# One logit block per attention chunk instead of two, with four of its eight products in the MLP's buffer, and two transpose groups in the first down phase

## The chip, the core and the metric

The kernel runs on one NeuronCore of a Trainium2 chip. The core has five engines, each with an instruction queue of its own that it works through in order: TensorE (PE: matmuls and transposes; the profile shows weight loads apart, as PEld), VectorE (DVE), ScalarE (ACT), GpSimd (POOL) and SyncE (SP). They wait for one another by semaphores. Matmuls read SBUF and write one of eight PSUM banks; ScalarE and VectorE carry results from PSUM to SBUF (an eviction). DMAs are issued from the queues of SP, POOL and ACT. The metric is the device time of one execution, in microseconds (us).

## The reference

It is one transformer block on x of 2048 x 576 (bf16), with layer norms modulated by a condition vector c:

```python
sa, ca, ga, sb, cb, gb = (silu(c) @ w_mod).reshape(6, 576)
h = layernorm(x) * (1 + ca) + sa
x = x + ga * attention(h, wqkv, wo)          # 32 heads of 18; 8 keys: positions s, s-2, ..., s-14
h = layernorm(x) * (1 + cb) + sb
x = x + gb * ((h @ w_gate) * (h @ w_up)) @ w_down   # 576 -> 4608 -> 576
```

Attention is local and dilated: a position looks at itself and at seven earlier ones, two apart. For each of the 8 offsets w the logits of a head are the sum over its 18 features of q times the shifted k; then a softmax over the 8, and the weighted sum of eight shifted v. Positions before the start are masked.

## The kernel before, in words

The 2048 positions are cut into eight chunks of 256 (`CH`). Chunks form the groups [0], [1, 2], [3, 4], [5, 6], [7] for the MLP. For each group TensorE goes through two phases. In the **gate/up** phase (`gate_up`) it computes, for each f of 36 slices of 128 hidden features, gate and up side by side, each on 64 rows of the array (class `Pair`, matmuls of L746, PSUM tiles `pg` and `pu`). ScalarE evicts them (L797, L798), and VectorE multiplies them into `hh` (L791, L800), which holds the hidden activations: 36 slices of 512 columns. In the **down** phase (`down`) it multiplies `hh` by w_down on the whole array (L961, L966), and the results go out.

Everything else is laid into these phases as background pieces, written as lists of tuples (TensorE time, VectorE time, what it needs, what it marks, how long the mark waits, what to call). The planner `timed` goes along the phase in estimated time and emits the next piece of a list as soon as its need is marked and VectorE's estimated backlog allows it. So the order of instructions on every engine is fixed when the kernel is built; the estimates only decide the order, and semaphores keep the data right. Pieces that don't fit go on into the following down phase (`late`).

While group g is in gate/up, the attention of the chunks of group g+1 runs beside it. For one chunk:

- `b_p` (L486, VectorE): a product, q times the shifted k, 128 x 1280 bf16, one per offset w. Products go to `prod_t`, which has room for four (`product`).
- `b_l` (L495, TensorE): a logit block for four offsets. 20 matmuls by the 0/1 matrix `ind` sum each head's features; four of them run side by side, each on 32 columns of the array. The result `lgT` (256 columns, half a PSUM bank) is copied by ScalarE to `lgs` (L498; a pool with two buffers).
- `b_ltd` (L512, SP queue): a DMA transpose of `lgs` into `lg_t`.
- `softmax_of` (VectorE and ScalarE), `values_of` (`b_mul`, `b_add`: eight multiplies and sums of the shifted v, into `o_sb`), `b_od` or `b_o`, which bring `o_sb` to `oT` by DMA transpose or by TensorE transposes (L561, evicted by ScalarE in L562, L563), and `b_w` (L642, L644), the output projection, which reads `oT`.

So a chunk has two logit blocks, for w = 0 to 3 and 4 to 7; the second four products reuse `prod_t` after the first block has read it. `prod_t` also serves the MLP: `ld_prods` loads two blocks of w_down into it for the down phase, on the POOL queue.

Group 0 is the special one. In its gate/up phase, near the end, stand two groups of ten TensorE transposes: `a_t4` (L333: `xn` of chunk 4 into `tr_pA`, `tr_pB`; ScalarE evicts three pieces into `hT` in L324, VectorE two in L322, and GpSimd then zeroes `hT`'s unused half in L423) and `b_o(1)` (`o_sb` of chunk 1 into `oT`). The down phase of group 0 is planned by `first_down`: it computes q, k and v of chunk 4 from `hT` (`a_q`, L441; `a_v`, L464), the output projection of chunk 1 from `oT`, then chunk 2's values and projection. Its lists start with a mark `h4` (hT ready, 1.5 after the start) and `o1` (oT ready, 1.5).

```python
product(n): k0 = (prod_n[0] % (4 * CH // n)) * KT * n
hhp.tile([P, FT * 2 * CH], BF, name="hh")     # 36 slices x 512 columns, made anew for each group
```

Of the kernel before, what the change touches and what calls it, by code (L numbers as in the profile page):

```python
# [7 lines left out]
BF = mybir.dt.bfloat16  # L8
F32 = mybir.dt.float32
# [9 lines left out]
P = 128  # L19
# [26 lines left out]
def kernel(  # L46
# [20 lines left out]
    def pool(name, bufs, **kw):  # L67
        return ctx.enter_context(tc.tile_pool(name=name, bufs=bufs, **kw))
# [8 lines left out]
    h2p = pool("h2p", 1)  # L77
    vstage = pool("vstage", 4)
    smp = pool("smp", 1)
    lgsp = pool("lgsp", 2)  # L80
    lgp = pool("lgp", 2)
    attnp = pool("attnp", 1)
    vshp = pool("vshp", 2)
# [337 lines left out]
    def a_t4():  # L421
        a_t(4, False)
        nc.gpsimd.memset(aa[4]["hT"][64:, KF, :], 0.0)  # L423
# [58 lines left out]
    def b_p(i, w):  # L482
        b = bb.setdefault(i, dict(prod={}, vsh={}))
        off = HALO - DIL * (W - 1 - w)
        prod = product(CH)
        nc.vector.tensor_tensor(prod, aa[i]["qT"][:], aa[i]["kT"][:, :, off:off + CH], ALU.mult)  # L486
        b["prod"][w] = prod

    def b_l(i, w0):
        b = bb[i]  # L490
        prods = [b["prod"].pop(w0 + c) for c in range(4)]
        lgT = ps([P, CH], F32, "lgT")
        for m in range(KT):
            for c in range(4):
                nc.tensor.matmul(lgT[H * c:H * (c + 1), :], lhsT=ind[:, m, :], rhs=prods[c][:, m, :],  # L495
                                 start=(m == 0), stop=(m == KT - 1), skip_group_check=True)
        lgs = lgsp.tile([P, CH], BF, name="lgs")
        nc.scalar.copy(lgs[:], lgT[:])  # L498
        b.setdefault("lgs", []).append(lgs)

    def b_lt(i):
        b = bb[i]
        b["lg"] = ps([P, ST, W, H], BF, "lg")
        for w0, lgs in zip((0, 4), b.pop("lgs")):
            for j in range(ST):
                nc.tensor.transpose(b["lg"][:, j, w0:w0 + 4, :].rearrange("p w h -> p (w h)"), lgs[:, js(j)], ident[:])

    def b_ltd(i, w0):
        b = bb[i]
        if w0 == 0:  # L510
            b["lg"] = lgp.tile([P, ST, W, H], BF, name="lg_t")
        b["ltd"] = nc.sync.dma_start_transpose(out=b["lg"][:, :, w0:w0 + 4, :].rearrange("p j w h -> p j (w h)"), in_=b["lgs"][w0 // 4][:])  # L512

    def b_exp(i):
        nc.scalar.activation(bb[i]["dd"][:], bb[i]["dd"][:], ACTF.Exp, scale=scale)
# [39 lines left out]
    def b_o(i):  # L555
        pA = ps([P, 4, CH], BF, "oT_pA")
        pB = ps([P, 1, CH], BF, "oT_pB")
        for m in range(KT):
            d = pA[:, m, :] if m < 4 else pB[:, 0, :]
            for j in range(ST):  # L560
                nc.tensor.transpose(d[:, js(j)], o_sb[:, j, m * P:(m + 1) * P], ident[:])  # L561
        nc.scalar.copy(oT[:, 0:4, :], pA[:])  # L562
        nc.scalar.copy(oT[:, 4, :], pB[:, 0, :])  # L563
# [117 lines left out]

    def prods_of(i):
        r = []
        for w in (0, 4):
            r += [(0, 0.82, "", f"p{i}{v}", 1.0, lambda v=v: b_p(i, v)) for v in range(w, w + 4)]
            r += [(0.75, 0, f"p{i}{w + 3}", f"l{i}{w}", 1.0, lambda w=w: b_l(i, w)), (0, 0, f"l{i}{w}", f"t{i}{w}", 9.0 if i == 7 else 6.0, lambda w=w: b_ltd(i, w))]
        return r
# [28 lines left out]

    def attention_of(c1, c2):
        p2, sm = prods_of(c2), softmax_of(c1)
        first = prods_of(c1) + p2[:4] + sm[:1] + p2[4:6] + sm[1:] + p2[6:]
        return first + values_of(c1, c2) + [(0, 0, "", "-", 0, lambda: b_od(c1))] + softmax_of(c2) + values_of(c2)  # L720

    def norm_of(n, after, free, load=None):
# [164 lines left out]
    def names(th):  # L887
        return [p[3] for p in th]
# [415 lines left out]
    def gb_row():  # L1304
# [27 lines left out]
    def first_down(late):  # L1332
        def q(g):
            return (0.53 if g == 2 else 1.07, 0, "h4", "-", 0, lambda: a_q(4, g))

        def v(j):
            return (1.2, 0, "h4", "-", 0, lambda: a_v(4, j))

        def out_1(first):
            return [(0, 0, "", "o1", 1.5, nop), (1.2, 1.35, "o1", "-", 0, lambda: b_w(1, 0)), (1.2, 1.35, "", "x1", 0.5, lambda: b_w(1, 1)),  # L1340
                    (0, 2.5, "", "s1", 0.7, lambda: b_ln(1)), (0, 0, "s1", "n1", 2.3, lambda: b_norm(1)), (0, 0, "n1", "t1", 9.5, lambda: b_td(1)),
                    (0, 1.0, "t1", "-", 0, lambda: (b_mod(1, (3, 4), False), b_mod(1, (0, 1, 2), True)))]
        a4 = [(0, 0, "", "h4", 1.5, lambda: ld_prods(0))]
        o2 = [(0, 0, "o21", "z2", 0.6, nop), (0.55, 0, "z2", "O2", 0.9, lambda: b_o(2)), (1.2, 1.35, "O2", "-", 0, lambda: b_w(2, 0)), (1.2, 1.35, "", "x2", 0.2, lambda: b_w(2, 1)),
              (0, 2.2, "", "s2", 0.7, lambda: b_ln(2)), (0, 1.5, "s2", "n2", 0.2, lambda: b_norm(2)), (0.55, 1.0, "n2", "-", 0, lambda: b_t(2))]
        return [a4, out_1(True), late + [(0, 0, "", "a2", 0.0, nop)] + values_of(2) + o2, [q(0), q(1), q(2), q(3), q(4), v(0), v(1)]]

# [61 lines left out]
```

## Time and profile before

Three runs: 541.29, 543.39 and 544.81 us; median 543.39.

| | |
|---|---|
| Profiled execution | 543.39 us, span 541.7 |
| TensorE busy | 534.3 us, 99% |
| VectorE, ScalarE, GpSimd busy | 316.6, 252.5, 70.7 us |
| Granted TensorE clock | 1.0 |
| Logit blocks' matmuls (L495) | 280, 10.4 us |
| Gate/up phase of group 0 ends, first down phase starts | 96.94 |
| First down phase ends | 127.51 |
| Gate/up phases of groups 1, 2, 3 | 127.51 to 208.20, 248.49 to 328.23, 368.51 to 446.72 |

Times inside an execution count from the start of the span. Lines of the timeline give start and duration of an instruction (or of several alike, merged, "x6"), engine, line of the kernel, operation, what it writes and reads, shapes, and in brackets how long the engine sat idle before it and what ended that. Matmuls are pipelined: one begins before the last one has ended, so what counts is from start to start. "64*128" or "128*32" before the shapes is the part of the array that a matmul uses, rows by columns.

### The profile page before, as it was taken

Reading aid. Unit: us, or ns where it says so; the run is one execution under the profiler, and the core shown is the slowest. Engines: PE = TensorE matmul, PEld = TensorE weight load, DVE = VectorE, ACT = ScalarE, POOL = GpSimd, SP = SyncE. Lnnn points to the kernel's source line nnn. Section 1 sums busy time; section 2 is a strip of 40 time slices with the busy share of each in tenths; the row PEclk is TensorE's granted clock in tenths of the full one; section 3 lists DMA queues with packets and bytes.
Section 4 is the critical chain, followed back from the end, with each engine's and each line's share of the span. In section 5 each row is a group of like instructions: output and inputs, shape, how many; then the busy total and the mean of one; then the engine's idle time right before and its main releaser. Section 6 shows DMA issues by size and latency. Waiting matters only on the chain.

```text
span 541.7 us, 14628 instructions
## 1 busy us (share of the span) xinstructions
PE 534.3 (99%) x6196; PEld 318.6 (59%) x6196; DVE 316.6 (58%) x715; ACT 252.5 (47%) x625; POOL 70.7 (13%) x110
## 2 busy tenths in 40 slices
PE   8999999999999999999999999999999999999997
PEld 4887888657745444555544444555544445558875
DVE  4899787758776768636358896534344924032212
ACT  4766877534656553012655552014555551006630
POOL 8104005012000210111000110110010101110210
PEclk9999999999999999999999999999999999999999
DMA  9999999879762794878344983983395592859730
GB/s 288 284 287 349 337 266 342 293 133 340 257 185 85 232 228 134 227 213 302 114 119 152 242 279 70 205 239 115 95 278 179 153 315 67 245 139 298 261 90 31
DMA packets 94978, 114.67 MB, mean 212 GB/s; under 512 B 28001, under 2 KB 83698, under 8 KB 94786
## 3 DMA queue, kind: packets, MB, share of 16 engines
q1 hardware_dynamic: 83184, 67.14, 44.7%
q0 software_dynamic: 11424, 46.40, 27.7%
q8 instruction: 48, 0.79, 0.6%
q10 hardware_dynamic: 306, 0.21, 0.1%
q14 instruction: 16, 0.13, 0.1%
HBM read 103.29 MB, written 4.74 MB: 199 GB/s over the span
## 4 chain that ended last, share of the span: by engine, by line
PE 97%; DMA 1%; DVE 0%; issue 0%; SPq 0%; ACT 0%
PE pg L746 29%; PE pu L746 23%; PE acc L961 20%; PE pq L441 4%; PE pq L746 3%; PE pw L644 3%; PE accr L966 3%; PE acc L1016 3%; PE lgT L495 2%; PE pv L746 2%; PE pv L464 2%; DMA wmA<-in_w_mod_dram 1%; PE po L599 1%; PE pwj L621 0%; PE accr L1019 0%; PE pwr L642 0%
## 5 line engine op out<-in xcount | busy, mean ns | idle before, releaser
L746 PE MATMUL pu<-h2T,wgu 64*128 64x512 bf16 (+1 forms) x1376 | 264.9, 331 | 0.9 <-issue 0.9
L746 PE MATMUL pg<-h2T,wgu 64*128 64x512 bf16 (+1 forms) x1376 | 265.7, 331 | 0.0
L746 PEld LDWEIGHTS <-wgu 64*128 64x128 bf16 x2752 | 133.9, 94 | 97.0 <-issue 1.1
L797 ACT CAST u_sb<-pu 128x512 bf16<-128x512 f32 (+1 forms) x172 | 85.8, 499 | 142.4 <-PE pg L746 142.2
L800 DVE TENSOR_TENSOR hh<-g_sb,u_sb 128x512 bf16<-128x512 bf16 x136 | 57.5, 424 | 116.2 <-ACT g_sb L798 115.3
L798 ACT CAST g_sb<-pg 128x512 bf16<-128x512 f32 (+1 forms) x172 | 86.8, 505 | 0.0
L961 PE MATMUL acc<-wd,hh 128*128 128x512 bf16 x344 | 86.1, 380 | 0.0
L961 PEld LDWEIGHTS <-hh 128*128 128x128 bf16 x504 | 49.0, 98 | 59.7 <-issue 1.3
L966 PE MATMUL accr<-wd,hh 128*128 128x64 bf16 x344 | 62.4, 193 | 0.0
L746 PE MATMUL pu<-h2T,wgr 64*128 64x512 bf16 (+1 forms) x188 | 61.5, 327 | 0.0
L746 PE MATMUL pg<-h2T,wgr 64*128 64x512 bf16 (+1 forms) x188 | 61.5, 327 | 0.0
L966 PEld LDWEIGHTS <-hh 128*128 128x128 bf16 x504 | 45.8, 98 | 1.9
L174 POOL DMA_DIRECT2D wd<-in_B_w_down_dram x29 | 21.9, 754 | 180.7 <-PE accr L966 100.1
L486 DVE TENSOR_TENSOR prod_t<-qT,kT 128x1280 bf16<-128x1280 bf16 x56 | 43.9, 820 | 1.3 <-ACT kT L817 0.7
L543 DVE TENSOR_TENSOR vsh<-vsh,attn 128x1152 bf16<-128x1152 bf16 x56 | 39.8, 752 | 0.0
L961 PE MATMUL acc<-prod_t,hh 128*128 128x512 bf16 x112 | 28.6, 380 | 0.0
L746 PEld LDWEIGHTS <-wgr 64*128 64x128 bf16 x376 | 18.5, 94 | 16.2 <-issue 3.0
L324 ACT ACTIVATE h2T<-h2T,modc 128x256 bf16<-128x256 bf16 x12 | 6.6, 595 | 41.5 <-DMA h2T<-xn 41.5
L480 POOL DMA_DIRECT2D vsh<-vd x14 | 12.6, 899 | 94.4 <-DVE o_sb L553 84.4
L441 PE MATMUL pq<-hT,wqk 128*128 128x256 bf16 (+1 forms) x225 | 21.7, 251 | 0.1
L746 PE MATMUL pq<-hT,wqk 64*128 64x256 bf16 (+1 forms) x360 | 21.7, 258 | 0.0
L966 PE MATMUL accr<-prod_t,hh 128*128 128x64 bf16 x112 | 21.6, 193 | 0.0
(214 smaller groups left out, 608.1 us busy)
## 6 DMA issues: line engine op xcount, KB each, us to landing
wgu<-in_B_w_gate_dram SPq DMA_DIRECT2D x41, 512.0 KB, 5.6
wgu<-in_B_w_up_dram SPq DMA_DIRECT2D x41, 512.0 KB, 7.1
wd<-in_B_w_down_dram POOLq DMA_DIRECT2D x29, 576.0 KB, 5.0
vsh<-vd POOLq DMA_DIRECT2D x14, 1152.0 KB, 9.8
prod_t<-in_B_w_down_dram POOLq DMA_DIRECT2D x8, 576.0 KB, 8.4
hh<-in_B_w_down_dram POOLq DMA_DIRECT2D x6, 576.0 KB, 7.3
x_t<-in_A_x_dram SPq DMA_DIRECT2D x8, 288.0 KB, 5.6
x_r<-in_A_x_dram SPq DMA_DIRECT2D x8, 288.0 KB, 7.8
```

Source lines behind the costliest of these rows:

```text
L174: return nc.gpsimd.dma_start(wb[:], B_w_down[r0:r0 + FB * P, :].rearrange("(k p) n -> p k n", p=P))
L441: nc.tensor.matmul(pq[:, gi, :], lhsT=wqk[:, kt, m * P:(m + 1) * P], rhs=hT[:, kt, cols], start=(kt == order[0] and not (by_k and gi)), st ...
L486: nc.vector.tensor_tensor(prod, aa[i]["qT"][:], aa[i]["kT"][:, :, off:off + CH], ALU.mult)
L543: nc.vector.tensor_tensor(v, v, at, ALU.mult)
L644: nc.tensor.matmul(pw[:], lhsT=oT[:, m, js(j)], rhs=wo[:, m, 0:512], start=(m == 0), stop=(m == KT - 1))
L746: return nc.tensor.matmul(out, lhsT=lhs, rhs=rhs, start=first, stop=last, skip_group_check=True)
L797: nc.scalar.copy(u[:, c, :], pu)
L798: nc.scalar.copy(g[:, c, :], pg)
L800: return lambda: nc.vector.tensor_tensor(hh[:, f - c:f + 1, :], g, u, ALU.mult)
L961: nc.tensor.matmul(acc[j][:], lhsT=hh[:, f, js(j)], rhs=wb[:, f % FB, 0:512], start=(f == 0), stop=(f == FT - 1))
L966: nc.tensor.matmul(accr[:, j, :], lhsT=hh[:, f, js(j)], rhs=wb[:, f % FB, 512:D], start=(f == 0 and j == 0), stop=(f == FT - 1), skip_grou ...
L1016: nc.tensor.matmul(acc[i][:], lhsT=hh[:, f, js(j)], rhs=wb(f)[:, c0:c1], start=(f == 0), stop=(f == FT - 1))
```

## The change

For chunks 3 to 7 there is one logit block of eight offsets. The products for w = 4 to 7 go to the last 5120 columns of `hh` (`room["hh"]`; slices 26 to 35 of the group that is in gate/up), so eight products can stand at once. `b_l` runs 40 matmuls into one `lgT` of 2 x 256 columns (one PSUM bank) and one copy to `lgs`, which is now one tile for both halves in a pool of one buffer. Both DMA transposes are issued one after the other behind it. The list of pieces has the chunk's softmax as a whole between the first four and the last four products of the group's second chunk. Chunks 1 and 2 keep two blocks, through the new `lgs` tile.

In group 0 the transposes `a_t4` and `b_o(1)` leave the gate/up phase; empty pieces with the marks `x4` and `O1` stay in their places. `a_t4`, with the load of x for chunk 6, now stands at the start of the first down phase in the same piece as `ld_prods(0)`, and `h4` is marked 1.7 after it; `b_o(1)` comes 0.4 after the start, and `o1` 1.9 after that. Chunk 2's `O2` waits 1.1 instead of 0.9.

The diff, by functions:

```diff
-    lgsp = pool("lgsp", 2)
+    lgsp = pool("lgsp", 1)
...
     def b_p(i, w):
-        prod = product(CH)
+        prod = product(CH) if i < 3 or w < 4 else room["hh"][:, (w - 4) * KT * CH:(w - 3) * KT * CH].rearrange("p (k n) -> p k n", k=KT)
...
-    def b_l(i, w0):
+    room = {}
+
+    def b_l(i, w0, quads=1):
         b = bb[i]
...
+        lgT = ps([P, quads, CH], F32, "lgT")
+        for q in range(quads):
+            prods = [b["prod"].pop(w0 + 4 * q + c) for c in range(4)]
+            for m in range(KT):
+                for c in range(4):
+                    nc.tensor.matmul(lgT[H * c:H * (c + 1), q, :], lhsT=ind[:, m, :], rhs=prods[c][:, m, :],
+                                     start=(m == 0), stop=(m == KT - 1), skip_group_check=True)
+        if w0 == 0:
+            b["lgs"] = lgsp.tile([P, 2, CH], BF, name="lgs")
+        nc.scalar.copy(b["lgs"][:, w0 // 4:w0 // 4 + quads, :], lgT[:])
...
     def prods_of(i):
         r = []
+        if i >= 3:
+            r = [(0, 0.82, "", f"p{i}{v}", 1.0, lambda v=v: b_p(i, v)) for v in range(W)]
+            return r + [(1.3, 0, f"p{i}7", f"l{i}", 1.2, lambda: b_l(i, 0, 2)), (0, 0, f"l{i}", f"t{i}4", 9.0 if i == 7 else 6.0, lambda: [b_ltd(i, w) for w in (0, 4)])]
...
     def attention_of(c1, c2):
-        first = prods_of(c1) + p2[:4] + sm[:1] + p2[4:6] + sm[1:] + p2[6:]
+        if c1 < 3:
+            first = prods_of(c1) + p2[:4] + sm[:1] + p2[4:6] + sm[1:] + p2[6:]
+        else:
+            first = prods_of(c1) + p2[:4] + sm + p2[4:]
...
-    first[at] = (0.6, 0, "o11", "-", 0, lambda: b_o(1))
+    first[at] = (0, 0, "o11", "O1", 0, nop)
...
-                                         (0.6, 0, "n4 v3", "x4", 0, lambda: (a_t4(), load_x(6)))],
+                                         (0, 0, "n4 v3", "x4", 0, nop)],
...
         def out_1(first):
-            return [(0, 0, "", "o1", 1.5, nop), (1.2, 1.35, "o1", "-", 0, lambda: b_w(1, 0)), (1.2, 1.35, "", "x1", 0.5, lambda: b_w(1, 1)),
+            return [(0, 0, "", "o0", 0.4, nop), (0.55, 0, "o0", "o1", 1.9, lambda: b_o(1)), (1.2, 1.35, "o1", "-", 0, lambda: b_w(1, 0)), (1.2, 1.35, "", "x1", 0.5, lambda: b_w(1, 1)),
...
-        a4 = [(0, 0, "", "h4", 1.5, lambda: ld_prods(0))]
+        a4 = [(0.6, 0, "", "h4", 1.7, lambda: (a_t4(), load_x(6), ld_prods(0)))]
...
+        room["hh"] = hh_t[:, FT * 2 * CH - 4 * KT * CH:]
```

As built, the changed order on TensorE has five blocks of 40 `lgT` matmuls for chunks 3 to 7; in the first down phase ten transposes of L333 after the first f, ten of L561 after the second, and the first `pq` of chunk 4 after the fourth. On POOL, ACT and DVE the moved evictions, the zeroing and the loads behind it follow at the same place; the eviction of chunk 2's first output half comes ahead of the modulation of chunk 1's `h2T` on VectorE.

More of the change, by code (lines that the diff above doesn't have):

```diff
@@ L484, in b_p @@
         off = HALO - DIL * (W - 1 - w)
-        prod = product(CH)
+        prod = product(CH) if i < 3 or w < 4 else room["hh"][:, (w - 4) * KT * CH:(w - 3) * KT * CH].rearrange("p (k n) -> p k n", k=KT)
         nc.vector.tensor_tensor(prod, aa[i]["qT"][:], aa[i]["kT"][:, :, off:off + CH], ALU.mult)
         b["prod"][w] = prod
-    def b_l(i, w0):
+    room = {}
+    def b_l(i, w0, quads=1):
         b = bb[i]
[L491 to L499, printed above, removed]
+        lgT = ps([P, quads, CH], F32, "lgT")
[8 more added lines that the diff above has]
+        nc.scalar.copy(b["lgs"][:, w0 // 4:w0 // 4 + quads, :], lgT[:])
     def b_lt(i):
@@ L503, in b_lt @@
         b["lg"] = ps([P, ST, W, H], BF, "lg")
-        for w0, lgs in zip((0, 4), b.pop("lgs")):
+        lgs = b.pop("lgs")
+        for w0 in (0, 4):
             for j in range(ST):
-                nc.tensor.transpose(b["lg"][:, j, w0:w0 + 4, :].rearrange("p w h -> p (w h)"), lgs[:, js(j)], ident[:])
+                nc.tensor.transpose(b["lg"][:, j, w0:w0 + 4, :].rearrange("p w h -> p (w h)"), lgs[:, w0 // 4, js(j)], ident[:])
     def b_ltd(i, w0):
@@ L511, in b_ltd @@
             b["lg"] = lgp.tile([P, ST, W, H], BF, name="lg_t")
-        b["ltd"] = nc.sync.dma_start_transpose(out=b["lg"][:, :, w0:w0 + 4, :].rearrange("p j w h -> p j (w h)"), in_=b["lgs"][w0 // 4][:])
+        b["ltd"] = nc.sync.dma_start_transpose(out=b["lg"][:, :, w0:w0 + 4, :].rearrange("p j w h -> p j (w h)"), in_=b["lgs"][:, w0 // 4, :])
     def b_exp(i):
@@ L1339, in out_1 @@
         def out_1(first):
-            return [(0, 0, "", "o1", 1.5, nop), (1.2, 1.35, "o1", "-", 0, lambda: b_w(1, 0)), (1.2, 1.35, "", "x1", 0.5, lambda: b_w(1, 1)),
+            return [(0, 0, "", "o0", 0.4, nop), (0.55, 0, "o0", "o1", 1.9, lambda: b_o(1)), (1.2, 1.35, "o1", "-", 0, lambda: b_w(1, 0)), (1.2, 1.35, "", "x1", 0.5, lambda: b_w(1, 1)),
                     (0, 2.5, "", "s1", 0.7, lambda: b_ln(1)), (0, 0, "s1", "n1", 2.3, lambda: b_norm(1)), (0, 0, "n1", "t1", 9.5, lambda: b_td(1)),
                     (0, 1.0, "t1", "-", 0, lambda: (b_mod(1, (3, 4), False), b_mod(1, (0, 1, 2), True)))]
-        a4 = [(0, 0, "", "h4", 1.5, lambda: ld_prods(0))]
-        o2 = [(0, 0, "o21", "z2", 0.6, nop), (0.55, 0, "z2", "O2", 0.9, lambda: b_o(2)), (1.2, 1.35, "O2", "-", 0, lambda: b_w(2, 0)), (1.2, 1.35, "", "x2", 0.2, lambda: b_w(2, 1)),
+        assert not {"O1", "x4"} & set(names(late))
+        a4 = [(0.6, 0, "", "h4", 1.7, lambda: (a_t4(), load_x(6), ld_prods(0)))]
+        o2 = [(0, 0, "o21", "z2", 0.6, nop), (0.55, 0, "z2", "O2", 1.1, lambda: b_o(2)), (1.2, 1.35, "O2", "-", 0, lambda: b_w(2, 0)), (1.2, 1.35, "", "x2", 0.2, lambda: b_w(2, 1)),
               (0, 2.2, "", "s2", 0.7, lambda: b_ln(2)), (0, 1.5, "s2", "n2", 0.2, lambda: b_norm(2)), (0.55, 1.0, "n2", "-", 0, lambda: b_t(2))]
```

## The prediction

> **What bounds the kernel now.** I read the page first: busy shares and the chain that ended last.
>
> ```profile
> PE 534.3 (99%) x6196; PEld 318.6 (59%) x6196; DVE 316.6 (58%) x715; ACT 252.5 (47%) x625; POOL 70.7 (13%) x110
> ...
> PE 97%; DMA 1%; DVE 0%; issue 0%; SPq 0%; ACT 0%
> ```
>
> TensorE is busy all the time and is the chain; its clock row shows 9s throughout. There is hardly a stall to remove: only TensorE's own time can shrink, or a new wait be added. So I went to TensorE's timeline and looked at what a foreign block costs inside the gate/up phase. First a logit block of chunk 7 (start, duration, engine, line):
>
> ```profile
> 391.56 0.38 PE L746 MATMUL pu<-h2T,wgu 64*128 64x512 bf16 x1
> 391.57 0.38 PE L746 MATMUL pg<-h2T,wgu 64*128 64x512 bf16 x1
> 391.87 0.73 PE L495 MATMUL lgT<-prod_t,ind 128*32 128x256 bf16 x20
> 392.54 0.39 PE L746 MATMUL pg<-h2T,wgr 64*128 64x512 bf16 x1
> ...
> 392.76 0.38 PE L746 MATMUL pg<-h2T,wgu 64*128 64x512 bf16 x1
> ```
>
> Gate and up matmuls start two by two every 0.215 us, but the block starts 0.305 after the last two: 0.09 lost going in. Its 20 matmuls run four side by side, so they are five steps of 256 columns. A 256-column matmul steps by 0.109 (10 of L441 take 98.91 to 100.00), which makes 0.545. The block takes 0.67: about 0.12 lost inside and coming out. Now ten transposes in gate/up, then ten in the first down phase:
>
> ```profile
> 90.83 0.27 PE L746 MATMUL pg<-h2T,wgu 64*128 64x256 bf16 x1
> 91.03 0.51 PE L333 MATMUL tr_pA<-shifts,xn 128*128 128x128 bf16 x6
> 91.38 0.39 PE L333 MATMUL tr_pB<-shifts,xn 128*128 128x128 bf16 x4
> 91.69 0.28 PE L746 MATMUL pg<-h2T,wgr 64*128 64x256 bf16 x1
> ```
>
> ```profile
> 118.99 0.19 PE L966 MATMUL accr<-prod_t,hh 128*128 128x64 bf16 x1
> 119.02 0.61 PE L561 MATMUL oT_pA<-shifts,o_sb 128*128 128x128 bf16 x8
> 119.47 0.28 PE L561 MATMUL oT_pB<-shifts,o_sb 128*128 128x128 bf16 x2
> 119.58 0.38 PE L961 MATMUL acc<-prod_t,hh 128*128 128x512 bf16 x1
> ```
>
> In gate/up, 90.83 to 91.69 is 0.86; less the 0.107 step of its own matmuls, the transposes cost 0.75. In the down phase the same ten cost 0.56, with no loss at either edge. The form column says what differs: gate/up works on 64 rows, the logit block on 32 columns, transposes and down matmuls on the whole 128*128 array. Each change of form costs about 0.1 us.
>
> **The change, part by part.**
>
> *One logit block per chunk (chunks 3 to 7).* The 40 matmuls stay, and one pair of edges goes. Two blocks cost 2 x (0.67 + 0.09) = 1.52, one costs 0.67 + 0.09 + 5 x 0.109 = 1.31: 0.21 saved, five times, 1.05.
>
> *Two transpose groups into the first down phase.* 0.75 - 0.56 = 0.19 to 0.20 each, 0.40 together. **TensorE's own time: -1.45.**
>
> [...] The trace shows about 0.1 per edge.
>
> *The hand-off in the first down phase is new.* Call its start T0 (before: 96.94). The timeline shows the evictions that move (91.66 to 94.45, with their durations), and the end of gate/up on VectorE and ScalarE, which they now stand behind:
>
> ```profile
> 91.66 1.49 ACT L324 ACTIVATE hT<-tr_pA,modc 128x256 bf16<-128x256 bf16 x3
> 91.80 0.73 DVE L322 TENSOR_SCALAR hT<-tr_pB,modc 128x256 bf16<-128x256 bf16 x2 [0.55 <-PE tr_pB L333]
> ...
> 92.64 0.31 POOL L423 MEMSET hT<- 64x256 bf16 x1 [1.23 <-PE pu L746]
> ...
> 93.54 1.06 ACT L562 COPY oT<-oT_pA 128x1024 bf16<-128x1024 bf16 x1
> ...
> 94.45 0.43 ACT L563 COPY oT<-oT_pB 128x256 bf16<-128x256 bf16 x1
> ...
> 96.53 0.43 DVE L800 TENSOR_TENSOR hh<-g_sb,u_sb 128x512 bf16<-128x512 bf16 x1 [2.01 <-ACT g_sb L798]
> ...
> 96.87 1.03 DVE L695 TENSOR_REDUCE ssum<-dd 128x64 f32<-128x512 f32 x1
> ...
> 97.94 0.26 ACT L696 ACTIVATE ssum<-ssum 128x64 f32<-128x64 f32 x1 [0.63 <-DVE ssum L695]
> ...
> 98.64 0.38 ACT L798 CAST g_sb<-pg 128x256 bf16<-128x256 f32 x1
> ```
>
> ScalarE's last g_sb ends at 99.02, T0 + 2.08: it stands behind chunk 2's softmax logarithm, which waits for VectorE. In the changed order the same instructions stand ahead of the moved evictions, so these start at T0 + 2.1. ScalarE's three hT pieces end at T0 + 3.5. VectorE's last hh (0.43) and two hT pieces (0.73) end at T0 + 3.2, and GpSimd's zeroing (0.11 after it, 0.31 long) at T0 + 3.6.
>
> TensorE meanwhile does one f of down matmuls (4, 0.49), hT's transposes (0.56), 0.49, oT's transposes (0.56), two more f (0.98), and arrives at pq at T0 + 3.08. Its third step needs the third piece at 3.30 and its fifth the zeroing at 3.52: about 0.2 late. Then oT: ScalarE's copies end at about T0 + 4.75 (1.06 and 0.43, overlapping a little), and TensorE wants the last of them at 3.08 + 0.2 + 1.09 + 0.12 = 4.5: 0.25 late. **Stall 0.45.** Bounds: 0, if the softmax sum is earlier because ScalarE no longer copies oT ahead of it, and 1.15, if the zeroing also waits for VectorE's next multiply (attn, 0.69). I take 0.45, which is what the rows give.
>
> Behind the waiting instructions: on GpSimd the two prod_t weight loads and one wd load, so they issue at about 99 to 100 instead of 93.14. prod_t is first read at 116.6 and its slowest landing in the trace took 13.5 us, so it is there by 113.4. DMA moved 355 GB/s or more until 105 and nothing from 107 to 109, so the delayed bytes close up. On ScalarE pq's copies are behind (before at 100.20, now about T0 + 4.8, also 100.2); on VectorE chunk 2's value multiplies, which end in o_sb at 116.5 and are next wanted at 119. VectorE's part of the h2T modulation now comes after one output block; it waits for a transpose landing at 123.2 anyway, and its reader is the next phase at 127.5. If any of this cover were gone, its delay would go straight into TensorE.
>
> *Products in hh's end, one lgs buffer, both DMA transposes together: nothing.* The eight multiplies keep their shape (0.82 each). The end of hh is read last in the previous down phase and written late in gate/up, long after the block. One 128x512 copy replaces two of 0.39. The pair of DMA transposes issues in 2 x 1.17, so the second is 1.17 later behind its block, but the softmax maximum that reads it comes well after: chunk 4 issued at 170.32 and was read at 187.52. The one place where VectorE waited for it (1.51, chunk 5, issued 274.58, read 280.42) gains, since that block now comes some 7 us earlier.
>
> *New wait: a block now needs all eight products.* TensorE stands in order behind it. Before, chunk 5's eighth product ended 265.4 because it waited for the first block; now it needs no such wait. By VectorE's order it ends at about 259.8, and the block starts 18 gate/up and 18 pq matmuls (1.94 + 0.98) after the old first one (259.38), at 262.3. Chunk 4: 166.4 against 168.85. The tightest was chunk 6, 288.8 against 289.69; its block comes one f (1.94) earlier, but its products stand one hh multiply earlier too. No stall expected.
>
> **Sum:** -1.45 + 0.45 = -1.0; with the bounds -1.45 to -0.3. The profiled execution took 543.39 (span 541.7 and 1.7 around it), which is also the median, so 542.4, and 541.9 to 543.1 by the bounds.
>
> **Rivals.**
> 1. *Only the way in is saved.* The 0.1 at the end of a block may be its last matmul running out, which any block pays. Then 7 x 0.09 = 0.63 goes and 0.45 comes: 543.2. Against it: in the down phase the transposes end without a tail.
> 2. *Slower: the zeroing on GpSimd.* It is on the path now. If it waits while VectorE does attn (0.69) and the next two multiplies (1.43), it ends at T0 + 3.2 + 2.1 + 0.3 = 5.6 and TensorE stalls 2.1: 543.39 - 1.45 + 2.1 = 544.0. It decides from a stall of 1.45 on. For it: nothing in the trace shows a zeroing beside such a multiply (at 92.64 a reduction ran). Against it: the order puts the zeroing right behind the eviction. [...]
> 3. *A block waits for its eighth product* in several chunks: if product order gains nothing while the block moves up by 1.94, chunk 6's margin of 0.87 becomes a stall of 1.07; in all five, 5.4, that is 543.39 - 1.0 + 5.4 = 547.8. Against it: VectorE sits idle for 1.0 to 2.6 us before most of its hh multiplies there (chunk 5's stretch), so it has room to be early.
> 4. *The merged block changes form between its halves*: 1.05 is not saved, 543.4.
>
> **How the numbers follow.** Forecast 0.68, rival 1 0.10, rival 2 0.12, rival 3 0.05, rival 4 0.05. Runs shown spread from 541.29 to 544.81, so a median can be off by over 1 us: 541.9 less 1.3 gives 540.6, and rival 2's 544.0 with 0.6 gives 544.6. About 1%, 5.4 us, is what a measurement tells from no change; TensorE idles 7 us in all, most of it outside the change, so faster by more is 0.01, slower (rival 3) 0.04, the same 0.95.
>
> **What would show it.** Logit blocks of 40 taking about 1.21 with 0.09 ahead, five of them; gate/up of the first group unbroken after pv; ten transposes at 0.56 in the first down phase; pq there starting some 0.2 late, pwr another 0.25. A gap over 1.45 there, or a wait of TensorE for VectorE at a block, proves me wrong.

## The result and the profile after

The changed kernel takes 540.8 us in the median of 20 runs (539.6 to 543.35), the kernel before 543.5 in the same measurement (541.24 to 544.81). The ratio is 0.9966 with a 95% interval of 0.9952 to 0.9980: 1.85 us less, 1.1 to 2.6. That is close to the difference of the means, 543.0 and 541.1; the medians differ by 2.7. Single runs of either kernel differ by 3.6 to 3.75 us; the last experiments show a part of where that comes from. Measured again (below), the ratio was 0.9976.

Three lines of the page of the changed kernel, its busy times, one DMA queue, and the chain that ended last:

```profile
PE 532.1 (99%) x6196; PEld 319.7 (59%) x6196; DVE 316.7 (59%) x715; ACT 252.6 (47%) x620; POOL 70.7 (13%) x110
...
q8 instruction: 48, 0.79, 0.6%
...
PE 97%; DMA 1%; DVE 0%; SPq 0%; ACT 0%; issue 0%
```

Queue q8 moves instructions, 48 packets and 0.79 MB; it comes up again further down. Nothing of the picture changed: the same 6196 matmuls, TensorE busy 99%, and TensorE is the chain. The profiled execution took 540.11 us (span 538.4), 3.3 less than the one before. To see where, I cut the timeline of TensorE into its phases, from the start of the first matmul of one to that of the next (us):

| | before | after | difference |
|---|---|---|---|
| set-up | 48.56 | 47.90 | -0.66 |
| gate/up of group 0, up to chunk 3's last v | 39.43 | 38.04 | -1.39 |
| the rest of it, where the transposes stood | 8.95 | 7.41 | -1.54 |
| first down phase | 30.57 | 31.96 | +1.39 |
| gate/up of groups 1, 2, 3 | 80.69, 79.74, 78.21 | 80.25, 79.30, 77.99 | -0.44, -0.44, -0.22 |
| all other phases | | | 0 to 0.01 |

Three rows are the change: -1.54, +1.39 and -1.10, together **-1.25**. The first two rows, -2.05, hold nothing that the change does to TensorE: its order there is the same, and matched matmul by matmul the two traces drift apart where matmuls wait for loads in the set-up, and at two gaps of before. One, at 62.2 inside a logit block, costs 0.25; the other is 1.2 us long in the middle of gate/up, at 69.4, where no engine is named as the cause:

```profile
69.42 0.27 PE L746 MATMUL pg<-h2T,wgu 64*128 64x256 bf16 x1
70.63 0.27 PE L746 MATMUL pu<-h2T,wgu 64*128 64x256 bf16 x1 [0.95 <-issue]
```

The trace after has neither gap. Why it had one and the other not is taken up in the last experiments.

Now the two places that the prediction spoke of. The logit block of chunk 7 after the change, on TensorE's timeline:

```profile
392.37 0.38 PE L756 MATMUL pu<-h2T,wgu 64*128 64x512 bf16 x1
392.37 0.38 PE L756 MATMUL pg<-h2T,wgu 64*128 64x512 bf16 x1
392.68 0.73 PE L498 MATMUL lgT<-prod_t,ind 128*32 128x256 bf16 x20
393.23 0.72 PE L498 MATMUL lgT<-hh,ind 128*32 128x256 bf16 x20
393.88 0.39 PE L756 MATMUL pg<-h2T,wgr 64*128 64x512 bf16 x1
```

The first 20 matmuls read `prod_t`, the second 20 the end of `hh`. They start 0.55 apart, five steps of 0.11, with nothing between the halves. The block begins 0.31 after the last gate/up pair, where pairs follow each other every 0.215, and takes 1.20 where two blocks took 0.67 each. All five blocks of 40 look like this.

And the hand-off in the first down phase, which now starts at T0 = 93.35:

```profile
93.05 1.03 DVE L702 TENSOR_REDUCE ssum<-dd 128x64 f32<-128x512 f32 x1
93.35 0.39 PE L971 MATMUL acc<-wd,hh 128*128 128x512 bf16 x1
...
93.85 0.50 PE L333 MATMUL tr_pA<-shifts,xn 128*128 128x128 bf16 x6
...
94.90 0.61 PE L565 MATMUL oT_pA<-shifts,o_sb 128*128 128x128 bf16 x8
95.09 1.49 ACT L324 ACTIVATE hT<-tr_pA,modc 128x256 bf16<-128x256 bf16 x3
...
95.58 0.72 DVE L322 TENSOR_SCALAR hT<-tr_pB,modc 128x256 bf16<-128x256 bf16 x2
...
96.22 0.68 DVE L710 TENSOR_TENSOR attn<-dd,rs 128x512 bf16<-128x512 f32 x1
96.41 0.31 POOL L423 MEMSET hT<- 64x256 bf16 x1 [6.36 <-PE oT_pB L565]
...
96.44 1.25 PE L441 MATMUL pq<-hT,wqk 128*128 128x256 bf16 x10
...
97.34 0.42 ACT L567 COPY oT<-oT_pB 128x256 bf16<-128x256 bf16 x1
...
97.54 0.48 PE L646 MATMUL pwr<-wo,oT 128*128 128x64 bf16 x5
...
97.85 1.24 PE L648 MATMUL pw<-wo,oT 128*128 128x512 bf16 x5
97.99 2.10 DVE L547 TENSOR_TENSOR vsh<-vsh,attn 128x1152 bf16<-128x1152 bf16 x3 [1.09 <-DMA vsh<-vd]
...
100.00 0.22 DVE L650 TENSOR_TENSOR x<-pwr,ga_bc 128x64 bf16<-128x64 f32 x1
100.02 0.31 PE L646 MATMUL pwr<-wo,oT 128*128 128x64 bf16 x5
...
100.27 1.24 PE L648 MATMUL pw<-wo,oT 128*128 128x512 bf16 x5
```

pq starts at T0 + 3.09 and takes 1.10, as it did before (1.09): it isn't late. Its third step comes at 96.66, 0.08 after ScalarE's third piece of hT; its fifth at 96.88, 0.16 after the zeroing. The first `pwr` and `pw` take 1.39 instead of 1.23, because the last step of `pwr` waits for ScalarE's copy that ends at 97.76: 0.16. The second pair takes 1.33 instead of 1.23, because `pw` waits for VectorE's `x<-pwr` of the first, which ends at 100.22, 0.05 before `pw` starts: 0.10. (In two traces below, where this wait is longer, the profile names that instruction.) That `x<-pwr` stands behind three value multiplies, and these waited 1.09 for a load, `vsh<-vd`. Before the change only two multiplies stood ahead of it.

### The profile page after: what moved, and what is told of

It is laid out like the page before. It is cut to its first block, busy times and chain, and to the rows that moved or that the text cites. A ratio compares the mean times of both kernels' runs of the same rounds, so it can differ in the third digit from the quotient of the medians.

```text
span 538.4 us, 14603 instructions
## 1 busy us (share of the span) xinstructions
PE 532.1 (99%) x6196; PEld 319.7 (59%) x6196; DVE 316.7 (59%) x715; ACT 252.6 (47%) x620; POOL 70.7 (13%) x110
## 4 chain that ended last, share of the span: by engine, by line
PE 97%; DMA 1%; DVE 0%; SPq 0%; ACT 0%; issue 0%
PE pg L756 29%; PE pu L756 23%; PE acc L971 20%; PE pq L441 4%; PE pq L756 3%; PE pw L648 3%; PE accr L976 3%; PE acc L1026 3%; PE pv L756 2%; PE pv L464 2%; PE lgT L498 2%; DMA wmA<-in_w_mod_dram 1%; PE po L603 1%; PE pwj L625 0%; PE pwr L646 0%; PE accr L1029 0%
## 5 line engine op out<-in xcount | busy, mean ns | idle before, releaser
L486 DVE TENSOR_TENSOR prod_t<-qT,kT 128x1280 bf16<-128x1280 bf16 x36 | 28.2, 818 | 3.5 <-ACT kT L827 2.7
```

## The experiments

Each was timed beside the kernel before. Phases are read from each trace as above. "Value multiply" is the start of chunk 2's first `vsh` multiply in the first down phase, counted from T0.

| kernel | ratio to before, 95% | gate/up of groups 1, 2, 3 | first down phase | value multiply |
|---|---|---|---|---|
| before | | 80.69, 79.74, 78.21 | 30.57 | 3.17 |
| after | 0.9966 (0.9952 to 0.9980) | 80.25, 79.30, 77.99 | 31.96 | 4.64 |
| logits only | 0.9965 (0.9941 to 0.9988) | 80.32, 79.30, 77.99 | 30.57 | 3.16 |
| moves only | 0.9985 (0.9966 to 1.0003) | 80.69, 79.74, 78.20 | 31.85 | 4.42 |
| eight products, two blocks | 0.9991 (0.9971 to 1.0011) | 80.69, 79.74, 78.21 | 31.86 | 3.58 |
| two blocks back to back | 0.9987 (0.9968 to 1.0006) | 80.25, 79.29, 77.99 | 31.85 | 4.29 |
| copy on VectorE | 0.9975 (0.9956 to 0.9995) | 80.25, 79.29, 77.99 | 32.11 | 4.79 |
| zeroing seven times | 1.0019 (0.9998 to 1.0040) | 80.25, 79.30, 77.99 | 33.76 | 4.25 |
| after, stream moved by 64 | 1.0019 (1.0001 to 1.0038) | 80.25, 79.30, 77.99 | 31.87 | 3.59 |
| before, stream moved by 64 | 1.0040 (1.0022 to 1.0059) | 80.69, 79.74, 78.20 | 30.57 | 3.16 |
| after, moved by 128 | 1.0006 (0.9987 to 1.0025) | 80.25, 79.30, 77.99 | 31.84 | 3.56 |
| before, moved by 128 | 1.0021 (1.0004 to 1.0038) | 80.69, 79.74, 78.20 | 30.57 | 3.16 |
| after, moved by 192 | 1.0021 (1.0000 to 1.0041) | 80.25, 79.30, 77.99 | 35.81 | 6.96 |
| after, again | 0.9976 (0.9956 to 0.9995) | 80.25, 79.30, 77.98 | 31.86 | 3.58 |

The ratios are uncertain by about 1 us, more than a single step of this change. The gate/up phases of groups 1 to 3 repeat to 0.02 wherever the order is the same, but for the 80.32 of logits only, so they decide between theories, and the ratios only say what all of it is worth.

### Each half of the change alone

Logits only: the transposes go back to the gate/up phase of group 0.

```diff
-    first[at] = (0, 0, "o11", "O1", 0, nop)
+    first[at] = (0.6, 0, "o11", "-", 0, lambda: b_o(1))
...
-                                         (0, 0, "n4 v3", "x4", 0, nop)],
+                                         (0.6, 0, "n4 v3", "x4", 0, lambda: (a_t4(), load_x(6)))],
...
-        a4 = [(0.6, 0, "", "h4", 1.7, lambda: (a_t4(), load_x(6), ld_prods(0)))]
+        a4 = [(0, 0, "", "h4", 1.5, lambda: ld_prods(0))]
...
```

The first down phase's list of the output projection, and `O2`'s 0.9, are those of before too.

> The changed kernel with both transpose groups put back into the gate/up phase of group 0; merged logit blocks stay. Edge theory: every merged block saves one pair of form changes, 0.21 us, so the gate/up phases of groups 1, 2 and 3 take 80.25, 79.29 and 77.99 us as in the changed kernel (80.69, 79.74 and 78.21 before), 1.1 less together, and the end of group 0 and its down phase take what they took before (8.95 and 30.57). Whole time 1.1 below the kernel before. Rival (the gain needs both parts, since the hand-off also moves group 1's start): groups 1 to 3 gain less than 0.9 together.

Moves only: the kernel before, with its two blocks per chunk, and the opposite edit.

```diff
-    first[at] = (0.6, 0, "o11", "-", 0, lambda: b_o(1))
+    first[at] = (0, 0, "o11", "O1", 0, nop)
...
-        a4 = [(0, 0, "", "h4", 1.5, lambda: ld_prods(0))]
+        a4 = [(0.6, 0, "", "h4", 1.7, lambda: (a_t4(), load_x(6), ld_prods(0)))]
...
```

> The kernel before with both transpose groups moved into the first down phase; two logit blocks per chunk as before. Edge theory: gate/up's end takes 7.41 instead of 8.95, the first down phase 31.96 instead of 30.57 (1.13 of transposes and 0.26 of waiting for the output projection's operand and bank), so 0.15 net, and groups 1 to 3 take 80.69, 79.74 and 78.21 as before. Whole time 0.1 to 0.2 below the kernel before, not to be told from none. Rival (the whole time fell by more than the phases show, so the moves gain elsewhere): 0.7 or more below the kernel before.

The two halves don't touch each other. Logits only gains 0.37, 0.44 and 0.22 in the three gate/up phases and leaves the first down phase at 30.57, as before. Moves only has the old gate/up phases, and group 0 as in the changed kernel: 7.41 for the rest of its gate/up, 31.85 for the down phase. So the moves are worth 1.54 - 1.28 = 0.26 us here, and 0.15 in the profiled run after, where the second output projection waited 0.10. The logit blocks carry the change: with them alone the median was 540.68, against 540.8 for all of it in another session.

### What in the merged block gains: the edges, VectorE's freedom or the bank

Eight products, two blocks: the products and the buffer as changed, but each half of the logits is its own block as soon as its four products are there.

```diff
-            r = [(0, 0.82, "", f"p{i}{v}", 1.0, lambda v=v: b_p(i, v)) for v in range(W)]
-            return r + [(1.3, 0, f"p{i}7", f"l{i}", 1.2, lambda: b_l(i, 0, 2)), (0, 0, f"l{i}", f"t{i}4", 9.0 if i == 7 else 6.0, lambda: [b_ltd(i, w) for w in (0, 4)])]
+            for w in (0, 4):
+                r += [(0, 0.82, "", f"p{i}{v}", 1.0, lambda v=v: b_p(i, v)) for v in range(w, w + 4)]
+                r += [(0.75, 0, f"p{i}{w + 3}", f"l{i}{w}", 1.2, lambda w=w: b_l(i, w))]
+            return r + [(0, 0, f"l{i}4", f"t{i}4", 9.0 if i == 7 else 6.0, lambda: [b_ltd(i, w) for w in (0, 4)])]
```

> The changed kernel, eight products and one copy target as there, but the logit block of chunks 3 to 7 in two pieces of 20 matmuls again, with gate/up work between. Edge theory: five pairs of edges come back, so groups 1 to 3 take 80.67, 79.71 and 78.20, 1.05 more than in the changed kernel. Rival (what gains is that products no longer wait for the first block to free their buffer): they stay within 0.2 of the changed kernel's 80.25, 79.29 and 77.99 together.

Two blocks back to back: one piece of the list, but two blocks of 20, each with its own bank and its own copy by ScalarE.

```diff
-            return r + [(1.3, 0, f"p{i}7", f"l{i}", 1.2, lambda: b_l(i, 0, 2)), (0, 0, f"l{i}", f"t{i}4", 9.0 if i == 7 else 6.0, lambda: [b_ltd(i, w) for w in (0, 4)])]
+            return r + [(1.3, 0, f"p{i}7", f"l{i}", 1.2, lambda: (b_l(i, 0), b_l(i, 4))), (0, 0, f"l{i}", f"t{i}4", 9.0 if i == 7 else 6.0, lambda: [b_ltd(i, w) for w in (0, 4)])]
```

> The changed kernel, but a chunk's 40 logit matmuls are two blocks of 20 that stand one right behind the other, each with its own PSUM bank and its own copy by ScalarE; nothing is left out. Theory (the gain is the change of the array's form, paid once per visit instead of twice): gate/up phases of groups 1 to 3 as in the changed kernel, 80.25, 79.30 and 77.99 us, at most 0.03 more each. Rival (the gain comes from the single bank and the single copy): they go back to 80.69, 79.74 and 78.21 as before. Median within 0.5 of the changed kernel's 540.8.

With two separate blocks all of the gain in gate/up is gone, to 0.01 us, although eight products stand at once and none waits for a block. The timeline of that kernel, chunk 7:

```profile
390.29 0.73 PE L498 MATMUL lgT<-prod_t,ind 128*32 128x256 bf16 x20
390.95 0.39 PE L758 MATMUL pg<-h2T,wgr 64*128 64x512 bf16 x1
...
396.88 0.73 PE L498 MATMUL lgT<-hh,ind 128*32 128x256 bf16 x20
397.55 0.39 PE L758 MATMUL pg<-h2T,wgr 64*128 64x512 bf16 x1
```

Each block pays its own way in and out: 0.66 from its start to the next gate/up matmul, for five steps of 0.11. With two blocks back to back all of the gain stays, in two banks and with two copies:

```profile
392.59 0.73 PE L498 MATMUL lgT<-prod_t,ind 128*32 128x256 bf16 x20
393.14 0.72 PE L498 MATMUL lgT<-hh,ind 128*32 128x256 bf16 x20
393.79 0.39 PE L756 MATMUL pg<-h2T,wgr 64*128 64x512 bf16 x1
```

The halves start 0.55 apart, like those of the one block. So what is saved is one change of form each way, 0.22 a chunk; the one bank and the one copy give nothing.

### The stall at the output projection

Copy on VectorE: the second copy of chunk 1's `oT` goes to VectorE.

```diff
-        nc.scalar.copy(oT[:, 4, :], pB[:, 0, :])
+        (nc.vector.tensor_copy if i == 1 else nc.scalar.copy)(oT[:, 4, :], pB[:, 0, :])
```

> The changed kernel, with the smaller of the two copies of chunk 1's oT in the first down phase (128x256) on VectorE instead of ScalarE. VectorE waits there until 97.99 for a load anyway. If the 0.16 wait of the first output projection in that phase is the queue of copies on ScalarE, it goes, and the first down phase takes 31.8 instead of 31.96; the second, 0.10, stays if it is the bank that VectorE frees late. If the wait is something else, 31.96 stays. Whole time 0.1 to 0.2 below the changed kernel, about 1.4 below the kernel before.

```profile
100.01 0.32 PE L646 MATMUL pwr<-wo,oT 128*128 128x64 bf16 x5
100.17 1.24 PE L648 MATMUL pw<-wo,oT 128*128 128x512 bf16 x5
...
102.34 0.31 PE L646 MATMUL pwr<-wo,oT 128*128 128x64 bf16 x5
...
102.62 0.22 DVE L650 TENSOR_TENSOR x<-pwr,ga_bc 128x64 bf16<-128x64 f32 x1
...
102.89 1.24 PE L648 MATMUL pw<-wo,oT 128*128 128x512 bf16 x5 [0.24 <-DVE x L650]
```

The first `pwr` takes 0.16 in this trace (100.01 to 100.17) where it took 0.31 in the changed kernel: its stall is gone, so ScalarE's copy was its cause. But the phase was longer, 32.11, where 31.8 was expected. The load of `vsh` landed later, 4.79 after T0, and the second `pw` waited for the `x<-pwr` behind the multiplies: it starts 0.55 after its `pwr`, 0.30 later than in the changed kernel (0.25) and 0.40 later than undisturbed (0.15); the profile counts 0.24 of that as idle. What the edit took away at one place was taken back at the other by a load that the edit doesn't touch.

### The price of a late zeroing

```diff
-        nc.gpsimd.memset(aa[4]["hT"][64:, KF, :], 0.0)
+        for _ in range(7):
+            nc.gpsimd.memset(aa[4]["hT"][64:, KF, :], 0.0)
```

> The changed kernel with the zeroing of hT's unused half on GpSimd done seven times over instead of once (same zeros). This prices the wait that the slower rival of the prediction rested on. In the changed kernel one zeroing took 0.31 us and was done 0.15 before pq's fifth step read it. Theory (a delay behind that slack is paid in full, and it swallows the 0.26 of the two later stalls at the output projection): seven end about 2.0 us later, the first down phase takes 31.96 + 1.85 - 0.26 = 33.5, the median is 542.0 to 542.6. Whoever holds that GpSimd's writes wait for VectorE's two-input multiplies expects the zeroings beside attn and the value multiplies to take well over 0.31 each and the phase over 34.5. Whoever holds that a stall there is made up later expects the phase within 0.3 of 31.96.

```profile
99.25 0.68 DVE L711 TENSOR_TENSOR attn<-dd,rs 128x512 bf16<-128x512 f32 x1
99.45 2.49 POOL L424 MEMSET hT<- 64x256 bf16 x7 [7.05 <-PE oT_pB L566]
...
100.64 2.10 DVE L548 TENSOR_TENSOR vsh<-vsh,attn 128x1152 bf16<-128x1152 bf16 x3 [0.70 <-DMA vsh<-vd]
...
101.99 0.81 PE L442 MATMUL pq<-hT,wqk 128*128 128x256 bf16 x6 [1.91 <-POOL hT L424]
```

Seven zeroings take 2.49, 0.36 each with the time between them, beside `attn` and two of the three value multiplies; these keep their 0.68 and 0.70. GpSimd was not held up by VectorE's two-input multiplies: the rival's mechanism doesn't show here. Its price does. The phase grew by 1.8 to 1.9 over 31.85 and 31.96, close to the 33.5 that full payment behind the slack gave; the median was 544.16, 1.6 us over the range expected. In the profiled execution (545.4) the excess lies outside this phase: it also has gaps of 1.7 us at 83.07 and 0.5 at 61.19 and 69.33.

### Where the gaps in group 0 come from

The traces name nothing for these gaps. But TensorE's instructions come by DMA as well, as the size of queue q8 tells: 48 packets, 0.79 MB, which is about 64 bytes for each of TensorE's 12,392 matmuls and weight loads, 256 to a packet of 16 KB. Counted along TensorE's stream, the gap at 69.42 before stands behind the 1985th instruction, that at 61.89 in the logits-only kernel behind the 1729th and that at 83.11 in the copy-on-VectorE kernel behind the 2497th: each the 193rd of 256. For the first of them, the DMA view of before from 66.1 to 66.2, which shows the packets that began in this tenth of a microsecond and their time as a share of it on 16 engines:

```profile
q8 instruction: 1, 0.02, 191.6%
```

1.916 x 16 x 0.1 = 3.07 us for this packet; the median one takes 1.1. It ended at 69.2, and TensorE went on 1.4 us later.

To test it, fillers of TensorE that stand in the first 6 us, where it waits for the first loads, were made smaller and more: `keep_busy(n, columns)` issues n matmuls that nobody reads, and `NB` is 512. That moves every later instruction along the packets, here by 64, and leaves the rest of the program as it is.

```diff
-    keep_busy(7, NB)
+    keep_busy(5, NB)
+    keep_busy(16, 64)
...
-    keep_busy(5, NB)
+    keep_busy(3, NB)
+    keep_busy(20, 64)
```

> The changed kernel with 32 more filler matmuls in the first 6 us (four of 512 columns replaced by 36 of 64), where TensorE waits for the first loads anyway; nothing else. It moves every later TensorE instruction by 64 places in its instruction stream. The traces show this stream coming by DMA in 48 packets of 16 KB, 256 instructions each, and every unexplained gap of TensorE so far stood at place 193 of 256 (1729th, 1985th or 2497th instruction), right behind a late packet. Theory (gaps are late instruction packets): the edge that fell into the fast logit block at about 61 us, with 2.5 us for its last 128 instructions, falls ahead of it, with 3.9; no gap over 0.25 there, and any gap elsewhere stands 64 instructions away from the old places, still at 193 of 256 of the new stream. The median is 539.6 to 540.6, with fewer runs over 541. Rival (the gaps belong to what the matmuls read): they stay at the same matmuls, and the median stays at 540.8, within 0.3.

> The kernel before with the same 32 more filler matmuls in the first 6 us. Theory (late instruction packets): as above, no gap in the logit block at about 61 us; median 541.5 to 542.6, where the kernel before has 543.2, and the difference to the shifted changed kernel is the 1.1 to 1.5 that the stages of the two traces show for the change itself. Rival: 543.2 as before, and the difference to the changed kernel stays 1.9.

In the logit block at 61 us neither trace has a gap; the changed kernel's had none there unmoved either. But both kernels became slower, by 2.5 and 1.5 us in the median, where I had expected them to become faster. The traces show one cause in both. After the change, stream moved by 64:

```profile
79.01 0.82 PE L756 MATMUL pq<-hT,wqk 64*128 64x256 bf16 x12
...
81.84 0.50 PE L756 MATMUL pq<-hT,wqk 64*128 64x256 bf16 x6 [2.01 <-issue]
```

Before, stream moved by 64:

```profile
79.41 0.89 PE L746 MATMUL pq<-hT,wqk 64*128 64x256 bf16 x12
82.08 0.39 PE L746 MATMUL pq<-hT,wqk 64*128 64x256 bf16 x4 [1.78 <-issue]
```

Both stop behind the 2497th instruction of the new stream, after 12 of 18 `pq` matmuls (the second view ends at 82.3). Unmoved, those 18 run through. In the first of the two, the packet began between 79.4 and 79.5, when TensorE had six instructions left, and took 1.16:

```profile
q8 instruction: 1, 0.02, 72.2%
```

So a gap follows the edge of a packet and not the matmul that stands there: it moved by 64 instructions when the stream did. What held this packet back isn't shown. Two 512 KB weight loads had been issued at 76.94 and 77.77, and I took them for the cause. A shift by 128 was to have this packet asked for ahead of such loads. That was tried in both kernels, and a shift by 192 in the changed one:

```diff
-    keep_busy(7, NB)
+    keep_busy(3, NB)
+    keep_busy(32, 64)
...
-    keep_busy(5, NB)
+    keep_busy(1, NB)
+    keep_busy(40, 64)
```

```diff
-    keep_busy(7, NB)
+    keep_busy(1, NB)
+    keep_busy(48, 64)
...
-    keep_busy(5, NB)
+    keep_busy(59, 64)
```

> The changed kernel with its TensorE stream moved by 128 instructions instead of 64 (8 filler matmuls of 512 columns in the first 6 us replaced by 72 of 64). With the shift by 64 the packet for the 2497th instruction began only 6 instructions ahead of its use, behind two 512 KB weight loads issued at 76.9 and 77.8, and TensorE stood 2.2 us. A shift by 128 puts that edge 3.5 us earlier still, so that its packet is asked for before those loads, when DMA moves 23 to 52 GB/s (74 to 76 us). Theory (a packet is late when it is asked for behind a bulk load): no gap of TensorE over 0.25 us from 60 to 105, median 539.6 to 540.8. Rival (the additional fillers themselves cost): 543.3 or more, as with 64.

> The kernel before with the same 128 instructions of fillers more. Theory: no gap over 0.25 from 60 to 105 either, median 541.0 to 542.0; against the changed kernel with the same shift, the difference is the change alone, 1.1 to 1.5 us by the stages. Rival (the change is worth the 1.9 that the medians differ by without a shift): 1.9 or more between the two.

> The changed kernel with its TensorE stream moved by 192 instructions (12 filler matmuls of 512 columns replaced by 108 of 64), the fourth quarter of a packet. One edge falls right behind the logit block of about 61 us (2.2 us for its last 128 instructions, the least of all four places), the others into plain gate/up stretches. Theory: gaps, if any, at place 193 of 256 of the new stream, the first of them after that block, 0.3 to 1 us; median 540.3 to 542.5, between the shifts by 128 and by 64. Rival (fillers cost by their number): above the shift by 64, over 543.3.

No place was better: medians of 543.1 and 543.8 for the changed kernel, 544.5 for the one before. Moved by 128, the changed kernel's trace has no gap at a packet's edge; the two that it has, 0.57 at 62.80 and 2.32 at 73.75 from start to start, are waits of TensorE for a load into `hh` and for `hT`, which waited for its DMA transpose. The trace of before, moved by 128, has no gap over 0.3 in group 0. So with this shift no packet came too late, but the medians didn't fall; what makes a packet late stays open. Moved by 192, the gap is in the first down phase, and it is the new wait of the change at full size:

```profile
100.80 2.10 DVE L547 TENSOR_TENSOR vsh<-vsh,attn 128x1152 bf16<-128x1152 bf16 x3 [3.45 <-DMA vsh<-vd]
102.81 0.22 DVE L650 TENSOR_TENSOR x<-pwr,ga_bc 128x64 bf16<-128x64 f32 x1
...
103.08 2.29 PE L648 MATMUL pw<-wo,oT 128*128 128x512 bf16 x5 [2.30 <-DVE x L650]
```

`vsh` landed 6.96 after T0, the second `pw` waited 2.30, and the phase took 35.81. So the theory of packets explains gaps at places 193 of 256, and not the scatter as a whole: in group 0, where DMA moved 207 to 369 GB/s in the 6 us windows from 60 to 102 before the change, packets are late now and then in traces of both kernels, and weights, a transpose and `vsh` in some of the changed one. Each profiled execution of the changed kernel that was moved holds one wait of 2.0 to 2.3 us and a halved clock behind it (last section; the mean granted clock is 0.997 in these three executions and 0.998 to 1.0 in the others); no other trace does. Why the added fillers make the median slower at all three shifts, in the kernel before too, is open; that they take time themselves is excluded by the set-up, 47.5 to 48.8 us in all traces.

### The changed kernel again

> The changed kernel itself once more, timed beside the kernel before. Theory (the change is worth what its stages show, 1.1 in the gate/up phases of groups 1 to 3 and 0.15 in group 0; the rest of the first difference of 1.85 was the loads' lateness in group 0, which differs from run to run in both kernels): gate/up phases 80.25, 79.30, 77.99 again, first down phase 31.85 to 32.0 if the shifted values of chunk 2 land by 4.6 us after its start and one us more for each us later; ratio 0.9965 to 0.9985. Rival (the change also takes away lateness in group 0): ratio at or under 0.9966 again, and no gap of TensorE over 0.4 us in group 0.

The ratio was 0.9976 (0.9956 to 0.9995), 1.3 us, about the sum of the phases; the first measurement's 1.85 has 1.3 in its interval. The phases came back, and the trace has gaps at three packet edges in group 0, of 0.29 to 0.44 from start to start (two records are missing ahead of the first, which makes it the 191st of 256 by count). So that the first trace of the changed kernel had none was no effect of the change.

## Why the prediction was right, and where its sizes were off

**The sum.** Predicted -1.0, 542.4 us; the change's phases show -1.25, the two measurements -1.85 and -1.3. The forecast's mechanism is what happened. The median of 540.8 lies 1.6 below the forecast: 0.25 of that is in the steps below, and the rest in the scatter that the range had allowed for. So the sum is right by its terms, and that the median came within the range, 0.2 from its end at 540.6, is in part luck.

**One logit block per chunk, -1.05:** measured -1.10. The 0.21 from one pair of edges measured 0.22, and two experiments tie it to the edges. The rivals that only the way in is saved and that the block changes form between its halves fall by the same lines. An edge costs 0.11 here, half of the 0.22.

**Transposes in the down phase, -0.40:** -1.54 in gate/up and +1.13 in the down phase, -0.41.

**The stall of 0.45: this is the term that was mis-sized.** Of the 0.2 at pq nothing came. ScalarE began the hT pieces at T0 + 1.74 and not 2.1. 0.23 of that came because VectorE's sum for the softmax stood earlier against the phase's start (T0 - 0.30, before T0 - 0.07), which the prediction had named as the reason for its lower bound; the rest because ScalarE began them 0.12 before its last g_sb had ended (95.09 and 95.21), where the prediction counted from the end. Then 0.16 instead of 0.25 at `pwr`, by the copy that was named. And 0.10 at a place that was not: the second `pw`.

**The queue that the prediction listed and read wrongly.** It named the value multiplies on VectorE as queued behind the waiting instructions, and asked when *they* are next wanted. It didn't ask what stands behind *them*: `x<-pwr`, which TensorE needs within 2 us. Before the change two multiplies stood ahead of it, with their load there in time (3.17 after T0 in all traces of the old order); now three, and the phase starts earlier against a load that doesn't. In the traces of the new order that load let the first multiply start between 3.56 and 6.96; up to 4.42 TensorE lost nothing, at 4.64 it lost 0.10, at 6.96 2.3 and the clock. The upper bound of 1.15 for the stall left this wait out and was too low.

**Slower by the zeroing:** refuted. One zeroing ran beside `attn` in 0.31, seven beside `attn` and value multiplies in 0.36 each.

**A block waits for its eighth product:** no block did. The least time from the last product to its block was 1.06 us, chunk 4's. Chunk 5's product and block came 11.3 and 13.8 us after their phase's start, the block 2.5 after the product, as predicted (259.8 and 262.3 by the old clock).

**The loads behind the zeroing on GpSimd** were issued at T0 + 3.56, and nothing waited for them, as predicted.

## What to carry to other kernels

A block with another tile form that is laid into a stream of matmuls pays for its edges, here 0.22 us a visit; put blocks of the same form next to each other before looking for anything finer. When work moves to an earlier place, list what stands *behind* each instruction that may now wait for a load, and who needs that; the load doesn't always move with it: here the multiply that waits for it started 3.17 after the phase did before the change, and 3.56 to 6.96 after it in the new order. And where single runs scatter more than the change is worth, cut the timeline into phases: here those of groups 1 to 3 repeat to 0.02 us where the medians differ by 1.

## What the runs showed of the hardware that was not expected

TensorE can run out of instructions, as two gaps tell: in the kernel before, behind the packet that took 3.07 us instead of 1.1, it was idle for 0.95, and in the changed kernel moved by 64, where a packet began six instructions ahead of its use, for 2.01. The profile calls both "issue".

A gap can also cost what comes after it. Windows of 1 us; the fields are length, busy time of PE, PEld, DVE, ACT and POOL, then TensorE's granted clock, DMA share and GB/s. The changed kernel moved by 192, after 2.30 us idle:

```profile
102.00:103.00 1.00, 0.00 (x0) 0.00 (x0) 1.00 (x4) 0.00 (x0) 0.00 (x0) 0.90 1.07 368
103.00:104.00 1.00, 0.92 (x3) 0.37 (x3) 0.97 (x3) 0.00 (x0) 0.00 (x0) 0.50 0.98 363
...
105.00:106.00 1.00, 1.00 (x5) 0.61 (x4) 0.59 (x1) 0.00 (x0) 0.00 (x0) 0.50 1.07 406
106.00:107.00 1.00, 1.00 (x11) 0.84 (x9) 0.97 (x4) 0.56 (x2) 0.00 (x0) 0.89 1.00 355
```

The clock is halved for 3.4 us (three windows at 0.50, a fifth of the two beside them): a wait of 2.3 us cost the phase 3.96. The same happened to the changed kernel moved by 64, after 2.01 us idle (0.50 from 83 to 85), for 3.4 us again, and moved by 128, after 2.06: there the ten `pq` matmuls behind the gap take 1.42, where twelve take 0.82 in the trace moved by 64, and the mean clock of the execution is 0.997 as in the other two. It did not after 1.78 in the kernel before moved by 64, nor after the 1.91 of the seven zeroings:

```profile
83.00:84.00 1.00, 1.00 (x24) 0.88 (x20) 0.27 (x1) 0.65 (x2) 0.00 (x0) 1.00 0.27 77
84.00:85.00 1.00, 1.00 (x22) 0.84 (x19) 1.00 (x3) 0.65 (x2) 0.07 (x1) 1.00 1.11 310
```

These are two windows of the kernel before moved by 64, behind its gap. Of the gaps so far, 2.01 us were enough and 1.91 were not.

But the length alone doesn't decide. Behind the last matmul of the kernel before, at 537.93, TensorE does nothing for 3.7 us to the end of the span, and the windows from 539 to 540 and from 540 to 541.7 are at 1.00. Behind that of the changed kernel, at 534.63, the window from 536 to 537 is at 0.85 and the rest at 0.50. Nor does the clock change where a gap ends. For the gap that ends at 103.08 the window from 102 to 103 is at 0.90 already; for the one that ends at 81.84 the window from 81 to 82 is at 1.00, and the next at 0.77. What decides is open.
